# Attention ahead of a routed expert layer on one core: masks as TensorE products, plain row maxima moved within SBUF, no GpSimd work in the loop, K loaded once, heads normed in pairs

## The chip, the core and the metric

The kernel runs on one NeuronCore of a Trainium2 chip. TensorE multiplies matrices from SBUF into PSUM, VectorE (DVE) and ScalarE (ACT) do the elementwise work, GpSimd (POOL) is a fourth engine, SyncE (SP) issues transfers. Each engine executes its own instructions in the order in which the program was written; semaphores order them against each other. The metric is the time of one execution in microseconds on the device; the median of three runs is compared.

## What is computed

The first part is causal attention mixed with a recurrent memory, for 4 batches, 8 heads, 576 rows, head width 64:

```
scores = scale * np.matmul(q, k.transpose(0, 1, 3, 2))
scores = np.where(causal, -1000000000.0, scores)
scores = scores - scores.max(-1, keepdims=True)
a = np.exp(scores)
a /= a.sum(-1, keepdims=True) + 1e-09
local = np.matmul(a, v)
mem_ret = np.einsum('bhsd,bhde->bhse', q_p, M_prev)
mem_norm = np.einsum('bhsd,bhd->bhs', q_p, z_prev)[..., None] + 1e-06
return (g * mem_out + (1 - g) * local).astype(np.float32)
```

Here `q_p` is elu(q)+1, `mem_out` is `mem_ret / mem_norm` and `g` a sigmoid per head. Its 2304x512 result goes through a router that gives each of 8 experts 288 tokens (two 512x1024 layers each), and through a last layer with three 512x768 matrices, a maximum and a 768x512 matrix. All is float32; because the router's choices hang on small differences, products are split into a rounded part (fp32r) and a remainder.

## The kernel before

The 32 heads are worked off in 16 pairs. Of each pair the loop loads K and Q transposed (`Kr`, `Qr`, 64 rows, each written twice to fill 128 partitions), `QN` (Q again, for the memory), `MZ`, `V` and `VT`. ACT or DVE round Q and K to fp32r (`QX`, `KX`, `KB`), POOL computes the remainders (L436 into `KX`, L440 into `QL`).

Per head there are two passes over the scores. In the S pass (L480, and L482 for the last 64 rows of both heads together) TensorE computes score rows into one of three PSUM banks `s`, and DVE takes each row's maximum over score plus mask with one custom instruction (L499). The nine columns of maxima of a pair go out to DRAM, transposed element by element (L536, `nmd`), and come back as a row of `QL` (L543, L544), all on SP's queue. In the T pass (L598, L599) TensorE computes the transposed scores less the maxima into one of two banks `t`, ACT takes the exponential into `PT` (L609), POOL sets the upper triangle of the diagonal blocks to 0 (L627), and TensorE multiplies `PT` with `V` into one bank `av` per head (L642; a float32 product is two instructions). DVE divides by the row sums (L660 to L667) and adds to the batch's `x` (L671). The memory's products (L691) and the router's share of V (L383) have one bank, `mem`, in turn. After four pairs `x` is stored to DRAM (L801), from a tile whose rows of 64 elements lie 72 apart. Between these tasks 24 pieces of the last layer's float64 weights are loaded and turned to float32 (`m2raw`, L827 to L837).

The order on every engine comes from a planner (`Plan.run`): each task has engines it can run on with a cost, tasks it depends on, buffers from rings (`BUFS`), and a key (10 per pair, with offsets from `PRIO`). The planner takes the task that can start first, by key among equals, and writes the program in that order. The S pass has the offset -71 with six `KX`, so it runs about three pairs ahead of the T pass. Routing and the expert layer are planned apart, after it.

## Time and profile before

| | |
|---|---|
| Time, median of 3 runs (lowest, highest) | 1027.08 us (1024.65, 1042.5) |
| The profiled execution: its own time / its span | 1036.35 us / 1034.4 us |
| Busy: PE, PEld, DVE, ACT, POOL | 93%, 86%, 60%, 30%, 21% |
| Mean granted TensorE clock | 0.827 |
| DMA | 97.60 MB in 73339 packets, 46218 of them under 512 bytes |

The span is from the first to the last instruction. Busy shares are sums over stages: attention takes the time up to 425 us, the expert layer most of what follows. [...] A busy PE is one whose matmuls overlap in the record; how fast they follow one another is read from their starts.

### The profile page before, as it was taken

To read this page: it belongs to the slowest core of one execution; us is meant where nothing else is said; L and a number is where in the kernel's file an instruction comes from. 1 tells how busy PE (TensorE), PEld (TensorE's weight loads), DVE (VectorE), ACT (ScalarE), POOL (GpSimd) and SP (SyncE) were. 2 spreads that over 40 slices of the span, in tenths; PEclk is the share of its full clock that TensorE was granted. 3 is DMA by queue.
4 is the path that set the end of the run, shared out by engine and by line. 5 is a ranking of instruction groups with operands and counts; after the bars stand their busy time and mean duration, and the time that the engine had idled before them with its cause. 6 is when DMAs were issued, how large, how long until landed. Compare 5 with 4: busy or idle time off the path is not lost.

```text
span 1034.4 us, 17357 instructions
## 1 busy us (share of the span) xinstructions
PE 962.2 (93%) x6570; PEld 889.9 (86%) x6570; DVE 619.5 (60%) x1724; ACT 314.6 (30%) x678; POOL 216.9 (21%) x299
## 2 busy tenths in 40 slices
PE   7789998899989999668899999999989999999997
PEld 5679897789778878558899999999989999999996
DVE  8546656557774753588874775857727736253321
ACT  5223333224342322412223224223123133242311
...
GB/s 229 143 128 116 129 171 73 161 116 133 149 130 122 126 92 18 47 114 74 82 86 119 88 6 161 43 65 141 3 75 143 3 136 71 44 163 1 41 2 31
DMA packets 73339, 97.60 MB, mean 94 GB/s; under 512 B 46218, under 2 KB 48266, under 8 KB 73256
## 3 DMA queue, kind: packets, MB, share of 16 engines
...
## 4 chain that ended last, share of the span: by engine, by line
PE 60%; issue 14%; DMA 13%; DVE 9%; POOL 1%; SPq 1%; ACT 1%; POOLq 0%; DVEq 0%; ACTq 0%
PE av L642 9%; PE w L1270 8%; PE w L1272 8%; PE w L1271 8%; DMA m2raw<-in_m2w 4%; PE acc L1271 4%; PE acc L1270 4%; PE acc L1272 4%; DMA Qr<-in_qT 3%; PE t L598 3%; PE t L599 2%; PE s L480 2%; PE mem L691 2%; DMA Kr<-in_kT 2%; PE rps L1018 1%
## 5 line engine op out<-in xcount | busy, mean ns | idle before, releaser
L642 PEld LDWEIGHTS av<-V,PT 128*128 128x128 f32 (+2 forms) x960 | 167.1, 256 | 17.1 <-issue 5.6
L642 PE MATMUL av<-V,PT 128*128 128x73 f32 (+2 forms) x960 | 176.5, 347 | 0.0
L1270 PE MATMUL w<-yh,mh 128*128 128x288 f32 x576 | 174.4, 303 | 0.0
L1272 PE MATMUL w<-yh,ml 128*128 128x288 f32 x576 | 170.3, 296 | 0.0
L1271 PE MATMUL w<-yl,mh 128*128 128x288 f32 x576 | 170.0, 295 | 0.0
L1270 PEld LDWEIGHTS w<-yh,mh 128*128 128x128 f32 x576 | 109.3, 190 | 3.1
L1271 PEld LDWEIGHTS w<-yl,mh 128*128 128x128 f32 x576 | 109.0, 189 | 2.9
L1272 PEld LDWEIGHTS w<-yh,ml 128*128 128x128 f32 x576 | 108.9, 189 | 0.0
L1241 DVE TENSOR_TENSOR wlo<-wraw,whi 128x1024 fp32r<-128x1024 f32 x64 | 80.2, 1254 | 41.3 <-ACT whi L1237 41.2
L609 ACT ACTIVATE PT<-t 128x512 f32<-128x512 f32 x96 | 54.7, 595 | 157.2 <-PE av L642 95.1
L1204 POOL DMA_INDIRECT xg<-xd,tidx x24 | 23.8, 992 | 372.7 <-PE w L1272 181.9
L499 DVE CUSTOM_DVE_ANT_0 junk<-s,mask 128x256 bf16<-128x256 f32 (+4 forms) x145 | 73.4, 508 | 46.7 <-PE s L480 38.7
L1375 DVE TENSOR_TENSOR mt<-w,mt 128x288 f32<-128x288 f32 x96 | 43.8, 456 | 80.2 <-PE w L1272 76.1
L598 PE MATMUL t<-QX,KX 128*128 128x512 f32 (+4 forms) x160 | 75.1, 475 | 6.7 <-ACT PT L609 6.7
L1271 PE MATMUL acc<-hl,whi 128*128 128x288 f32 x256 | 77.6, 303 | 3.1 <-DVE hl L1178 2.7
L1270 PE MATMUL acc<-hh,whi 128*128 128x288 f32 x256 | 77.4, 302 | 2.8 <-ACT hh L1172 2.8
L1237 ACT CAST whi<-wraw 128x1024 fp32r<-128x1024 f32 x64 | 66.8, 1049 | 39.0 <-PE acc L1271 22.2
L1272 PE MATMUL w<-xhi,wlo 128*128 128x288 f32 x256 | 76.7, 300 | 1.1 <-DVE wlo L1241 1.1
L1270 PE MATMUL w<-xhi,whi 128*128 128x288 f32 x256 | 77.2, 301 | 0.0
L1271 PE MATMUL w<-xlo,whi 128*128 128x288 f32 x256 | 76.7, 299 | 0.0
L1272 PE MATMUL acc<-hh,wlo 128*128 128x288 f32 x256 | 76.3, 298 | 0.0
L627 POOL TENSOR_SCALAR_AFFINE_SELECT PT<-PT 128x256 f32<-128x256 f32 (+1 forms) x96 | 45.0, 476 | 148.5 <-ACT PT L609 137.6
...
## 6 DMA issues: line engine op xcount, KB each, us to landing
...
```

The lines of the kernel that those rows point to most:

```text
L499: V.tensor_tensor_reduce(out=junk[ps_, :z - a], in0=o.s[ps_, :z - a], in1=mask[ps_, k:k + z - a], scale=-0.125, scalar=init, op0=OP.add, o ...
L598: nc.tensor.matmul(o.t[:kr, c:c + z - a], r.KX[i][:, ks], r.QX[i][:, a:z], start=True, stop=False)
L609: A.activation(u.PT[:kr, at0:at0 + wd], o.t[:kr, :wd], AF.Exp, scale=0.125)
L627: G.affine_select(v, v, pattern=[[1, m]] if cnt == 1 else [[0, 2], [1, m]], compare_op=OP.is_ge, fill=0.0, base=0, channel_multiplier=-1)
L642: nc.tensor.matmul(av[:m, j], u.PT[:kr, o:o + m], r.V[:kr, kb, i], start=(kb == 0), stop=(kb == j))
L1204: g.gather = G.indirect_dma_start(out=x.xg[:96, c], out_offset=None, in_=xd, in_offset=bass.IndirectOffsetOnAxis(ap=r.tidx[:96, c:c + 1], ...
L1237: A.copy(x.W[fb][0], x.RAW[fb])
L1241: V.tensor_sub(x.W[fb][1], x.RAW[fb], x.W[fb][0].bitcast(F32))
L1270: nc.tensor.matmul(o, wh, rh, start=start, stop=False)
L1271: nc.tensor.matmul(o, wh, rl, start=False, stop=False)
L1272: nc.tensor.matmul(o, wl, rh, start=False, stop=stop)
L1375: V.tensor_max(q.mt, o.pt[:, :T], q.mt)
```

## The change

The attention part is written anew; routing and experts stay. Per pair and no longer per head:

- Masks: before each diagonal score product TensorE multiplies a bf16 identity with a bf16 mask into the same bank and the score product adds to it (L394, L403 in the S pass, L556 in the T pass). POOL's selection in `PT` is gone.
- Row maxima: DVE takes them with plain maximum reductions (L413), nine per pair, and one maximum joins the two parts of the last rows (L436). TensorE transposes the nine columns (L440), ACT copies them to SBUF and issues three transfers on its own queue that write them into the row of `QL` (L449, L450). The pass through DRAM is gone.
- `Kr` has 64 partitions and is loaded once; ACT rounds it (`KX`, `KB`) and Q, both heads in one instruction; DVE computes the remainders of both heads in one instruction each (L353, L358). POOL keeps one small copy per pair (`MZ`).
- Both heads have one buffer `av` of two banks; the division is done for both at once (L617 to L632). The memory's part of `x` is scaled by ACT, ten instructions per pair (L532). `x` is kept without the router's eight columns, which have a tile `g` of their own, so that the store's rows are 512 elements.
- The rings are shorter (`KX` 3, `QX` 3, `KB` 2 for pairs) and the S pass runs one pair ahead.

```diff
-PRIO = {'load': -12, 'phi': 2.0, 'min2': ['ACT'], 'prep': 7.5, 'cpe': ['ACT', 'DVE'], 'sube': ['POOL'], 'S': -71.0, 'J4': -2.0, 'R': -78.0, 'E': 29.0, 'N': -37.5, 'T': -3.0, 'A': 18.5, 'M': -60.0, 'rowe': ['ACT'], 'maske': ['POOL'], 'norm': 0.5, 'xadd': ['DVE'], 'mem': [0, 9], 'gate': 45.5, 'G': -13.0, 'gev': ['ACT'], 'm2': [15.0, 2, 25.0]}
+PRIO = {"load": -14, "prep": -12, "cb": 3, "S": -11, "N": -11, "nmte": "ACT", "G": -4, "phi": -6, "mem": (-2, -1), "memx": "ACT", "T": 0, "E": 0, "A": 4,
+        "norm": 4, "gate": -9, "m2": (4.0, 6.3, 6.0)}
...
-                for a in range(2):
-                    nc.sync.dma_start(t[64 * a:64 * a + 64], src[b, pp])
+            tK.append(load("Kr", [64, 2, S], kT[b, pp], k0 - 3 * (p == 0) + .01 * u, 1400 // len(parts), a, z, 1, u == 0))
...
-                copy(e, r.KX[i], r.Kr[:, i])
-                vg(e).tensor_sub(r.KX[i][64:], r.Kr[64:, i], r.KX[i][64:].bitcast(F32))
+                copy(e, r.KX[:64, s], r.Kr[:, s])
+                V.tensor_sub(r.KX[64:, s], r.Kr[:, s], r.KX[:64, s].bitcast(F32))
+                V.tensor_sub(r.QL[:64, s], r.Qr[:64, s], r.QX[:64, s].bitcast(F32))
...
-                V.tensor_tensor_reduce(out=junk[ps_, :z - a], in0=o.s[ps_, :z - a], in1=mask[ps_, k:k + z - a],
-                                       scale=-0.125, scalar=init, op0=OP.add, op1=OP.min, accum_out=acc)
+                        PE.matmul(o.s[:, c + z - a - 128:c + z - a], identb, ms[:, :128], start=True, stop=False,
+                                  skip_group_check=True)
+                        PE.matmul(d, r.QX[:, i, 128 * j:128 * j + 128], r.KX[:, i, a:z], start=False, stop=True,
+                                  skip_group_check=True)
+                    V.tensor_reduce(r.nm[:, col:col + k], o.s[:, c:c + k * w].rearrange("p (k w) -> p k w", k=k), axis=AX.X, op=OP.max)
...
-                nc.sync.dma_start(nmd[p].rearrange("c p -> p c"), u.nr.bitcast(F32))
-                    nc.sync.dma_start(q[:, :512], nmd[p:p + 1, 4 * i:4 * i + 4].rearrange("o c p -> o (c p)"))
-                    nc.sync.dma_start(q[:, 512:], nmd[p:p + 1, 8, 64 * i:64 * i + 64])
+            PE.matmul(r.pn[:9, :128], r.nm[:, :9], identr, start=True, stop=True)
+            copy(e, r.nmt, r.pn[:9, :128])
+            for i in range(2):
+                A.dma_start(q[:, i, :512], r.nmt[4 * i:4 * i + 4])
+            A.dma_start(q[:, :, 512:], r.nmt[8:9].rearrange("o (i q) -> o i q", i=2))
...
+                if diag:
+                    PE.matmul(o[:kr, c:c + kr], identb[:kr, :kr], mt[:kr, :kr], start=True, stop=False, skip_group_check=True)
...
-                    G.affine_select(v, v, pattern=[[1, m]] if cnt == 1 else [[0, 2], [1, m]], compare_op=OP.is_ge,
-                                    fill=0.0, base=0, channel_multiplier=-1)
...
+                for a in range(k):
+                    for i in range(2):
+                        A.mul(x[:, a, i], mv[:, a, i, :64], u.rm[:, a, i:i + 1])
...
-                    nc.sync.dma_start(xd[r].rearrange("p (h c) -> p h c", h=H), x[:rows(j), j, :, :64])
+                    nc.sync.dma_start(xd[r], x[:rows(j), j].rearrange("p h c -> p (h c)"))
```

How the order on TensorE changes, in the middle of the attention (`s`: S pass, `t`: T pass, `av`: PT times V, `mem`: memory and router products; sizes are partitions x columns). Before:

```order
L642 MATMUL av_108<-V,PT 128x73 x10
L691 MATMUL mem<-MZ,phi 128x146
L691 MATMUL mem<-MZ,phi 64x146
L642 MATMUL av_108<-V,PT 64x73 x5
L642 MATMUL av_109<-V,PT 128x73 x3
L480 MATMUL s<-KX,QX 128x128
L642 MATMUL av_109<-V,PT 128x73 x3
L480 MATMUL s<-KX,QX 128x256
L691 MATMUL mem<-MZ,phi 128x146 x3
L480 MATMUL s<-KX,QX 128x384
L598 MATMUL t<-QX,KX 128x320
L599 MATMUL t<-QL,KB_126 128x320
```

The products of the four kinds alternate. Now, from the end of one pair's `av` products to the first scores of the pairs behind it:

```order
L591 MATMUL av<-V,PT 128x73 x4
L591 MATMUL av<-V,PT 64x73 x5
L462 MATMUL mem<-wb,VT 128x16 x4
L462 MATMUL mem<-wb,VT 64x16
L591 MATMUL av<-V,PT 128x73 x10
L591 MATMUL av<-V,PT 64x73 x5
L509 MATMUL mem<-MZ,phi 128x146 x3
L394 LDWEIGHTS identb
L394 MATMUL s<-mask_s,identb 128x128
L396 MATMUL s<-KX,QX 128x512
L394 LDWEIGHTS identb
L394 MATMUL s<-mask_s,identb 128x128
```

Both heads' `av` products stand together, and the memory, S and T products, with the masks among them, stand together behind them. The T pass of the next pair follows a few rows on, also without `av` products between:

```order
L396 MATMUL s<-KX,QX 128x384
L556 LDWEIGHTS identb
L556 MATMUL t<-mask_t,identb 128x128
L557 MATMUL t<-QX,KX 128x512
L558 MATMUL t<-QL,KB_129 128x512
L557 MATMUL t<-QX,KX 128x64
L558 MATMUL t<-QL,KB_129 128x64
L556 LDWEIGHTS identb
L556 MATMUL t<-mask_t,identb 128x128
L557 MATMUL t<-QX,KX 128x448
L558 MATMUL t<-QL,KB_129 128x448
```

On SP's queue, before, at the end of a batch: the maxima's way through DRAM and the store of `x` stand among the loads, which wait behind them.

```order
L342 DMA QN<-in_qN 128x576
L536 DMA nmd<-nmr 128x9x1
L801 DMA xd<-x 1024x1x64 x4
L801 DMA xd<-x 512x1x64
L817 DMA m2raw<-in_m2w 128x1024
L543 DMA QL<-nmd 1x512
L544 DMA QL<-nmd 1x64
```

Now only loads and the store, in rows of 512 elements, are left on SP:

```order
L323 DMA Qr<-in_qT 64x1152 x2
L735 DMA m2raw<-in_m2w 128x1024
L717 DMA xd<-x 128x512 x4
L717 DMA xd<-x 64x512
L323 DMA MZ<-in_mz 128x146
L323 DMA V<-in_v 128x730
```

The maxima's transfers are now on ACT, behind the copy that they wait for, with the exponentials of the pair at work around them:

```order
L577 ACTIVATE PT<-t 128x512
L290 COPY nmt<-s 9x128
L532 ACTIVATE x<-mem,rm 128x64 x4
L449 DMA QL<-nmt 1x4x128 x2
L450 DMA QL<-nmt 1x2x64
L290 CAST qj_131<-Qr 128x2x64
L575 ACTIVATE PT<-t 64x2x64
```

Whatever stands behind these three on ACT, casts of the next pair and exponentials, is issued after them.

## Rows read from the trace of the kernel before

**Rows 1.** Busy time by stretch, attention: PEclk granted clock, DMA share, GB/s.
```profile
core 0: us, PE busy (x) PEld busy (x) DVE busy (x) ACT busy (x) POOL busy (x), PEclk, DMA share, GB/s
36.00:425.00 389.00, 361.29 (x1764) 320.69 (x1763) 226.38 (x646) 117.01 (x247) 131.31 (x186) 0.61 0.66 115
```
**Rows 2.** The same view, four shorter stretches of the attention.
```profile
120.50:164.80 44.30, 44.30 (x187) 39.59 (x186) 25.70 (x78) 13.18 (x30) 14.13 (x17) 0.50 0.64 136
250.20:267.20 17.00, 16.31 (x126) 14.53 (x124) 16.54 (x44) 8.61 (x18) 7.65 (x11) 1.00 1.08 160
265.00:270.00 5.00, 3.65 (x29) 3.05 (x28) 4.97 (x9) 2.17 (x5) 3.94 (x4) 1.00 0.98 206
396.00:416.00 20.00, 20.00 (x90) 17.79 (x91) 4.48 (x13) 4.10 (x9) 2.63 (x6) 0.50 0.00 0
```
**Rows 3.** The same view, the eight stretches at full clock: first, and their sum.
```profile
113.60:120.50 6.90, 6.43 (x52) 5.75 (x52) 6.52 (x16) 4.31 (x10) 4.46 (x6) 0.99 0.89 235
...
sum 85.50, PE 70.14 PEld 61.29 DVE 66.88 ACT 34.61 POOL 38.89; mean PE 8.77 PEld 7.66 DVE 8.36 ACT 4.33 POOL 4.86
```
**Rows 4.** Timeline of DVE: start us, us; division at a head's end (one per head).
```profile
63.63 0.52 DVE L667 TENSOR_TENSOR tmp<-av,r 128x360 f32<-128x360 f32 x1
...
119.32 0.53 DVE L667 TENSOR_TENSOR tmp<-av,r 128x360 f32<-128x360 f32 x1
...
144.74 0.53 DVE L667 TENSOR_TENSOR tmp<-av,r 128x360 f32<-128x360 f32 x1
...
254.80 0.53 DVE L667 TENSOR_TENSOR tmp<-av,r 128x360 f32<-128x360 f32 x1
...
263.87 0.52 DVE L667 TENSOR_TENSOR tmp<-av,r 128x360 f32<-128x360 f32 x1
...
424.93 0.53 DVE L667 TENSOR_TENSOR tmp<-av,r 128x360 f32<-128x360 f32 x1
```
**Rows 5.** Timeline of PE at either clock level.
```profile
102.51 1.82 PE L642 MATMUL av<-V,PT 128*128 128x73 f32 x8
104.07 0.45 PE L480 MATMUL s<-KX,QX 128*128 128x128 f32 x1
104.32 1.47 PE L691 MATMUL mem<-MZ,phi 128*128 128x146 f32 x4
...
114.88 1.01 PE L642 MATMUL av<-V,PT 128*128 128x73 f32 x8
115.70 0.30 PE L480 MATMUL s<-KX,QX 128*128 128x128 f32 x1
```
**Rows 6.** Busy time of L1217 (bf16 128x128 products, one after another) by stretch.
```profile
452.00:454.80 2.80, 2.80 (x29) 2.80 (x27) 0.50 1.09 41
455.20:458.00 2.80, 2.80 (x54) 2.80 (x52) 1.00 0.52 40
```
**Rows 7.** Groups by line and shape: count, busy us, mean ns; idle before, releasers.
```profile
L499 DVE CUSTOM_DVE_ANT_0 junk<-s,mask 128x512 bf16<-128x512 f32 x42 | 28.8, 685 | 15.5 <-PE s L480 9.3 <-PE s L482 6.0
L667 DVE TENSOR_TENSOR tmp<-av,r 128x360 f32<-128x360 f32 x32 | 16.9, 529 | 0.4
L609 ACT ACTIVATE PT<-t 128x512 f32<-128x512 f32 x90 | 51.2, 595 | 155.2 <-PE av L642 95.1 <-PE t L599 56.3 <-PE av L598 3.8
L406 DVE SCALAR_TENSOR_TENSOR phi<-QN,ph 128x576 f32<-128x576 f32 x2 | 1.5, 742 | 0.0
```
**Rows 8.** Timeline: a DVE and a POOL instruction that ran at one time.
```profile
264.83 1.41 POOL L440 TENSOR_TENSOR QL<-Qr,QX 64x576 fp32r<-64x576 f32 x1 [1.02 <-PE av L599]
264.88 1.98 DVE L406 SCALAR_TENSOR_TENSOR phi<-QN,ph 128x576 f32<-128x576 f32 x1
```
**Rows 9.** SP's queue: timeline, and waits of 36 to 425 us (total, times, longest).
```profile
256.55 10.62 SPq L801 DMA_DIRECT2D xd<-x  x5
...
SPq L543 <- DMA nmd<-nmr: 80.2, 13, 9.9
```
**Rows 10.** Timeline of PE just ahead of the clock's rise at 113.6 us.
```profile
109.93 1.76 PE L691 MATMUL mem<-MZ,phi 128*128 128x146 f32 x6
```

681 lines of the change are left out of this document (299 added, 382 removed).

## The prediction

> **What bounds the kernel now.** I read the busy times by stretch first, then the division at each head's end as a mark of pace, then TensorE's and DVE's timelines, then waits.
>
> Attention lasts to about 425 us; no line behind it changes, so its 609 us (1034.4 - 425) stay. From 36 to 425 us no engine is full except PE: 361 of 389 us busy at a granted clock of 0.61, DVE 226, ACT 117, POOL 131 [rows 1]. The mean hides two regimes [rows 2]. [...] The eight full-clock stretches sum to 85.5 us, 22% of the 389 [rows 3].
>
> The division at a head's end gives the pace [rows 4]: 25.4 us per pair at half clock (119.32 to 144.74), 9.07 us per head or 18.1 per pair at full (254.80 to 263.87), and 24.09 per pair over the fifteen pairs from 63.63 to 424.93. That is what has to shrink.
>
> **The change, part by part (per pair).**
>
> *TensorE.* Work goes up. Eight diagonal score blocks and one last pair block get a mask product in the S pass, ten blocks in the T pass: 19 products. The trace has no bf16 product among these. Nearest below are the bf16 128x128 products of the expert layer: 2.80 us / 29 = 0.097 us at half clock, 2.80 / 54 = 0.052 at full [rows 6]. Nearest above is the fp32r score product of 128 columns, which starts 0.25 us ahead of the next instruction at half clock [rows 5]. Each mask stands between products that load other weights, so I lean from the lower bound upward: 0.15 and, by the ratio below, 0.08. That is +2.9 us (1.8 to 4.8) at half clock and +1.5 at full; the transposition of the maxima adds 0.1. Eight `av` products take 104.07 - 102.51 = 1.56 us at half and 115.70 - 114.88 = 0.82 at full [rows 5], a ratio of 0.526. PE's work per pair is then 25.4 + 3.0 = 28.4 us at half clock (27.3 to 30.3) and 25.4 x 0.526 + 1.6 = 15.0 at full.
>
> *DVE.* Nine reductions of 3136 columns in all replace the custom maxima; POOL's two remainders come to DVE; the casts of K and Q leave it. From 360 elements in 529 ns, 512 in 685 (from PSUM) and 576 in 742 [rows 7] an instruction costs about 160 ns + 1.02 ns per element. Reductions: 9 x 0.16 + 3.2 = 4.6, and 0.2 for the maximum that joins two. Remainders: two of 1152, 2.7. Division and additions for both heads: 1460 elements in five instructions, 2.3. `phi` 0.75; the memory's divisors, six small ones, 1.1; 1.5 weight pieces of three instructions of 512, 3.1. Sum 14.8 us. Before it was 226.38 / 16 = 14.1, part of it stretched by POOL: 1.98 us for the `phi` instruction that ran beside L440 [rows 8], against 742 ns alone [rows 7]. That stretch goes.
>
> [...]
>
> *ACT.* 117.01 / 16 = 7.3 now [rows 1]. It takes all of the K and Q casts: 3456 columns at 595 ns per 512 [rows 7] are 4.0 at most, and about half of them were its own before, so +2. Ten scalings of 64 columns lie between 595 x 64 / 512 = 0.07 and 0.595 us each, 0.7 to 6.0; such a narrow one is mostly fixed cost, like DVE's 0.16, so I take 0.21 each, 2.1. The copy of the maxima 0.25. What three issues of transfers hold ACT no row shows; from nothing to 0.5 each, I take 0.25, 0.75. Sum 12.4, at the upper bounds 17: then ACT would be the bound at full clock, near the 17.5 below.
>
> *SP and DMA.* The store of `x` held SP's queue 10.6 us per batch, and the waits for the maxima's way out summed to 80.2 us in 13 [rows 9]; loads stood behind both. Both leave. K's second copy goes (64 x 1152 floats, 0.29 MB per pair). Where PE is the bound this is worth nothing now; it feeds the full-clock stretches, where the DMA share was 1.08 [rows 2].
>
> *The maxima's hop.* The three transfers are on ACT behind the copy; casts and exponentials are queued behind them, and the first remainder product of the T pass waits for them. The S pass is one pair ahead, and the 40 `av` instructions of the pair between give a cover of 40 x 0.195 = 7.8 us at half clock, 4.1 at full [rows 5], and the memory and score products on top. A hop of 2 to 3 us (an estimate from 6.2 us per wait for the hop through DRAM, which has two legs [rows 9]) is hidden. Were it not, 3 us x 15 pairs = 45 us come back.
>
> **The sum.** If the clock stayed as it is at half, the change loses 28.4 - 25.4 = 3 us per pair. At full clock the largest of PE 15.0, DVE 14.8, ACT 12.4 bounds a pair; with the waits that three nearly equal engines cause on each other I take 17.5 (18.1 was the best before). So the result hangs on f, the share of attention's time at full clock: a pair lasts P = 1 / (f / 17.5 + (1 - f) / 28.4). Attention changes by 15 x (P - 24.09); before, f was 0.22.
>
> | f | P | change | time |
> |---|---|---|---|
> | 0 | 28.4 | +65 | 1092 |
> | 0.22 | 25.0 | +13 | 1040 |
> | 0.50 | 21.7 | -36 | 991 |
> | 0.75 | 19.4 | -70 | 957 |
> | 1 | 17.5 | -99 | 928 |
>
> The profiled run took 1036.35 us (1034.4 span and 2 around it), 0.9% above the median 1027.08; I work the change out in its trace and take it from the median.
>
> Why f should rise: the order now puts memory, score, mask and T products of a pair in one stretch, and the `av` products, whose inputs lie ready, in another. Before, the clock rose at 113.6 us, 2 us behind a run of memory products [rows 10], while in 396 to 416 us, mostly `av` and T in turn, with PE busy 20.00 of 20.00 and no DMA at all, it stayed at 0.50 [rows 2]: a busy PE alone did not bring the rise there, and what stood ahead of one was such a run. It fell where PE waited for DVE, POOL or loads [rows 2]; these waits shrink, since POOL's share, SP's waits and DRAM leave the chain. Against: DVE and ACT have more work each, three engines are near equal at full clock, and PE will still wait. I take f = 0.5.
>
> **Rivals.**
>
> 1. *The clock rises half of the time* (f from 0.40 to 0.75): 957 to 1007 us. For it: the above. Chance 0.40; point 990.
>
> 2. *Full clock nearly throughout* (f over 0.75): 928 to 957. For it: no more SP or POOL waits. Against: DVE at 14.8 us of 17.5 leaves little slack, and each wait of PE was followed by a fall. Chance 0.20. [...]
>
> 3. *The clock stays as it is* (f from 0.19 to 0.40): masks and clock about cancel, 1007 to 1045. For it: PE was full before without the clock rising. Chance 0.18.
>
> 4. *The hop of the maxima is late*: the gain of f = 0.5 is eaten by 45 us, about 1035. For it: ACT issues it between exponentials, in its order. It decides from 2.4 us per pair on. Chance 0.07.
>
> 5. *Slower* (f under 0.19): TensorE has 3 us more per pair and its work is what bounds at half clock; if the waits at pair ends keep it there, 1047 to 1092. The point from which this decides is f = 0.19, close to the 0.22 of before. Chance 0.15.
>
> About 2% (20.5 us) is what a measurement of this kernel can tell from no change. Faster by more (f over 0.40 without a late hop): 0.60. Within: 0.25. Slower: 0.15. The range reaches from f = 0.93 (935) to f = 0.18 (1048), which leaves about 0.09 below and 0.11 above.
>
> **What would show it.** The granted clock of the attention (0.61 before): 0.75 at f = 0.5. The pace of the division: 21 to 22 us per pair; 28 in stretches at 0.50, 17 to 18 at 1.00. A reduction of 512 columns near 0.69 us; if it takes twice that, DVE is the bound at 19 us. A mask product 0.10 to 0.25 us ahead of its score product at half clock. No store over 5 us and no wait on `nmd` on SP. T's products with `QL` waiting on transfers would show rival 4, ACT at 15 us per pair a wrong price of its issues or scalings. I am wrong in kind if the clock share is about as before and the time still falls by 30 us, or if it rises and the time does not fall.

## The result: 930 us, under the range

The changed kernel takes 930.34 us (median of 4 runs, 928.14 to 935.49). The runs of before that stood beside them have a median of 1034.79 us; the ratio is 0.9076, with a 95% interval of 0.901 to 0.9142. The prediction said 990, with a range of 935 to 1048. The time is 60 us under the point and 5 us under the range. A single execution of these kernels can take a few per cent longer at a lower granted clock (before, on the chip of e14: 1066 to 1073 us at 0.79 to 0.81, beside 1046 to 1051 us at 0.82 to 0.83); the differences below are taken between executions without this. It lies where rival 2 was put ("full clock nearly throughout", 928 to 957, chance 0.20).

The profiled execution took 935.49 us with a span of 933.8, against 1034.4: 100.6 us less. The table shows where they went; the marks are the first instruction of the program, the division that ends pair 0, the division that ends pair 15, and the end.

| stretch | before, us | after, us | difference |
|---|---|---|---|
| start to the end of pair 0 | 63.6 | 55.2 | -8.4 |
| fifteen pairs | 361.3 (24.09 each) | 272.5 (18.17 each) | -88.8 |
| behind attention | 609.5 | 606.0 | -3.4 |

The sums are from [rows 4] and from these rows, the division on DVE now (start us, us, instruction; one per pair, and one per head for the last pair):

```profile
55.24 0.91 DVE L624 TENSOR_TENSOR tmp<-av,r 128x720 f32<-128x720 f32 x1
...
94.29 0.91 DVE L624 TENSOR_TENSOR tmp<-av,r 128x720 f32<-128x720 f32 x1
111.47 0.91 DVE L624 TENSOR_TENSOR tmp<-av,r 128x720 f32<-128x720 f32 x1
128.77 0.91 DVE L624 TENSOR_TENSOR tmp<-av,r 128x720 f32<-128x720 f32 x1
...
327.76 0.53 DVE L624 TENSOR_TENSOR tmp<-av,r 128x360 f32<-128x360 f32 x1
```

At full clock a pair lasts 17.2 us (94.29 to 111.47, and again to 128.77). Busy time by stretch of the changed kernel answers [rows 1] and [rows 2]: the whole attention, 20 us at full clock, and one of the falls.

```profile
core 0: us, PE busy (x) PEld busy (x) DVE busy (x) ACT busy (x) POOL busy (x), PEclk, DMA share, GB/s
36.00:331.00 295.00, 289.97 (x2099) 244.02 (x2099) 196.59 (x474) 175.84 (x409) 8.46 (x46) 0.90 0.49 143
...
100.00:120.00 20.00, 20.00 (x156) 16.13 (x155) 15.78 (x40) 13.71 (x32) 0.20 (x1) 1.00 0.66 194
160.00:166.60 6.60, 6.60 (x33) 6.08 (x32) 2.66 (x5) 2.70 (x4) 0.00 (x0) 0.50 0.39 113
```

The granted clock of the attention, as a share of full speed, is 0.90 where it was 0.61. The records of before and after have two levels of it, 0.50 (44.30 us at a stretch in [rows 2]) and 1.00 (the 20.00 us above), so the share of time at full clock is f = 2 x clock - 1: 0.80 now, 0.22 before. PE is busy 289.97 of 295 us, and 20.00 of 20.00 at full clock, where before it waited (3.65 of 5 in [rows 2]). The DMA share fell from 0.66 to 0.49 while the rate rose from 115 to 143 GB/s. That last pair of numbers turned out to be the clue.

### The profile page after: what moved, and what is told of

The parts are those of the page before. It is cut to its first block, busy times and chain, and to the rows that moved or that the text cites. A ratio compares the mean times of both kernels' runs of the same rounds, so it can differ in the third digit from the quotient of the medians.

```text
span 933.8 us, 17447 instructions
## 1 busy us (share of the span) xinstructions
PE 889.8 (95%) x6880; PEld 811.5 (87%) x6880; DVE 572.9 (61%) x1481; ACT 365.2 (39%) x826; POOL 80.0 (9%) x145
## 4 chain that ended last, share of the span: by engine, by line
PE 76%; issue 14%; DVE 4%; POOL 1%; DMA 1%; ACT 1%; ACTq 1%; SPq 1%; POOLq 0%; DVEq 0%
PE av L591 12%; PE w L1187 9%; PE w L1189 9%; PE w L1188 9%; PE acc L1188 4%; PE acc L1187 4%; PE acc L1189 4%; PE t L557 4%; PE mem L509 3%; PE t L558 3%; PE s L396 3%; PE rps L935 2%; PE mem L462 1%; PE t L556 1%; PE s L400 1%
## 5 line engine op out<-in xcount | busy, mean ns | idle before, releaser
L591 PE MATMUL av<-V,PT 128*128 128x73 f32 (+2 forms) x960 | 128.4, 286 | 1.6 <-ACT PT L575 0.7
L591 PEld LDWEIGHTS av<-V,PT 128*128 128x128 f32 (+2 forms) x960 | 116.1, 194 | 9.0 <-ACT PT L575 1.5
L1292 DVE TENSOR_TENSOR mt<-w,mt 128x288 f32<-128x288 f32 x96 | 43.6, 454 | 80.2 <-PE w L1189 78.0
L577 ACT ACTIVATE PT<-t 128x512 f32<-128x512 f32 x96 | 56.6, 609 | 87.0 <-PE t L558 85.8
L1154 ACT CAST whi<-wraw 128x1024 fp32r<-128x1024 f32 x64 | 66.8, 1049 | 40.3 <-PE acc L1188 22.2
L413 DVE TENSOR_REDUCE nm<-s 128x1 fp32r<-128x512 f32 (+4 forms) x160 | 69.1, 471 | 13.9 <-PE s L396 11.7
L1054 ACT CAST gc<-mt 128x32 fp32r<-128x32 f32 (+2 forms) x72 | 17.5, 243 | 143.4 <-DVE mt L1292 143.4
L557 PE MATMUL t<-QX,KX 128*128 128x512 f32 (+2 forms) x192 | 70.0, 366 | 0.0
L1095 DVE SCALAR_TENSOR_TENSOR hl<-w,hh 128x288 fp32r<-128x288 f32 x64 | 29.0, 455 | 63.3 <-ACT hh L1089 61.3
```

The source lines that it names most:

```text
L413: V.tensor_reduce(r.nm[:, col:col + k], o.s[:, c:c + k * w].rearrange("p (k w) -> p k w", k=k), axis=AX.X, op=OP.max)
L557: PE.matmul(d, r.KX[:, i, ks_], r.QX[:, i, a:z], start=not diag, stop=False, skip_group_check=True)
L577: A.activation(r.PT[:, items[0][0], out:out + 512], o.t, AF.Exp, scale=0.125)
L591: PE.matmul(av[:m, i, j], r.PT[:kr, i, o:o + m], V4()[:kr, kb, i], start=kb == 0, stop=kb == j)
L1095: V.scalar_tensor_tensor(lo(), src(), 0.0, hi().bitcast(F32), op0=OP.max, op1=OP.subtract)
L1154: A.copy(x.W[fb][0], x.RAW[fb])
```

## Where the loss of before sat, read again

Busy time of before by short stretches, about one of the stores of the maxima (issued by SP at 207.6 us), and a stretch without one:

```profile
204.00:208.00 4.00, 4.00 (x19) 3.91 (x18) 4.00 (x9) 0.81 (x2) 3.37 (x6) 0.50 0.53 114
208.00:212.00 4.00, 4.00 (x22) 3.64 (x21) 0.96 (x4) 0.00 (x0) 0.38 (x1) 0.50 1.10 9
212.00:216.00 4.00, 4.00 (x20) 3.75 (x19) 2.16 (x8) 1.66 (x3) 0.41 (x1) 0.50 0.56 34
248.00:252.00 4.00, 4.00 (x28) 3.76 (x27) 2.69 (x9) 0.69 (x1) 1.84 (x2) 0.73 0.98 287
```

From 208 to 212 us the DMA engines' mean busy share is 1.10 and they move 9 GB/s; from 248 to 252 nearly the same share (0.98) moves 287. The store transposes 9 x 128 values element by element, so it is 1152 writes of 4 bytes. The packets recorded from 208 to 210, from 210 to 219 and from 219 to 222 us:

```profile
DMA packets 1178, 0.03 MB, mean 13 GB/s; under 512 B 1168, under 2 KB 1168, under 8 KB 1178
DMA packets 120, 0.23 MB, mean 25 GB/s; under 512 B 10, under 2 KB 10, under 8 KB 120
DMA packets 421, 0.84 MB, mean 282 GB/s; under 512 B 53, under 2 KB 181, under 8 KB 420
```

The single elements are recorded within two us; for the nine us behind them the larger packets of the transfers issued next move at 25 GB/s, and then at 282. How the store holds up what comes behind it, the record does not show. The chain of waits of before, from 205 to 225 us (start us, us, what), shows what that costs TensorE:

```profile
208.72 12.84 DMA m2raw<-in_m2w
...
221.66 0.09 ACT m2a L827
...
222.24 0.59 ACT PT L609
222.83 0.04 issue
222.87 0.42 PE t L598
```

and the row of PE's timeline that it leads to, with the like rows at two other falls:

```profile
35.47 2.21 PE L383 MATMUL mem<-wb,VT 128*128 128x16 f32 x10 [1.10 <-DVE x L710]
177.37 0.85 PE L691 MATMUL mem<-MZ,phi 128*128 128x146 f32 x2 [3.33 <-ACT V L292]
222.87 0.42 PE L598 MATMUL t<-QX,KX 128*128 128x64 f32 x1 [2.09 <-ACT PT L609]
```

A weight piece issued at 208.7 us lands after 12.84 us. ACT is idle for 7.30 us ahead of L827, which reads it; the exponential L609, next in ACT's order, starts 0.58 us behind L827's start, and the T product that needs its bank starts behind that. PE was idle for 2.09 us there, and at 223 us the clock, which had been at full for 3.5 us, fell to 0.50. So a late load of the last layer's weights, which attention does not need at all, stopped attention, and the clock then stayed at half for 27 us (to 250) although PE was busy again, 27.20 of 27.20 us from 222.90 to 250.10. Of the eight falls after 36 us in the attention of before, five stand where ACT waited for a load: 3.3 to 7.6 us for a weight piece (192, 223, 318 and 370 us), 4.2 us for `V` (175, where PE was idle for 3.33 us). Two stand behind 1.36 us of PE's waiting for DVE's L710 (271 and 305), and one behind 0.47 us (120). A ninth, at 35 us, stands behind 1.10 us of waiting for L710.

By the full-clock stretches that [rows 3] adds up, the clock was at half for 303.5 of the 389 us: 151 us behind the five falls at a late load, 78 behind the fall at 35 us, 48 behind the one at 120, and 27 behind the other two. So half of the half-clock time begins at a late load. Why the clock then stays at half for tens of us under a busy PE, no run here shows.

The group of L827 and its counterpart, over the attention (count, busy us, mean ns, idle before it us and what ended it), before and after:

```profile
L827 ACT ACTIVATE m2a<-m2raw 128x512 f32<-128x512 f32 x24 | 16.2, 676 | 34.9 <-DMA m2raw<-in_m2w 30.2 <-DMA m2raw<-in_m2wo 4.5
```

```profile
L745 ACT ACTIVATE m2a<-m2raw 128x512 f32<-128x512 f32 x24 | 16.5, 687 | 0.6 <-DMA m2raw<-in_m2w 0.6
```

34.9 us of idle ACT became 0.6.

## The experiments

Four theories stood at first: A, the order on TensorE brings the clock (the prediction's); B, TensorE no longer waits for others; C, the mask products themselves lift the clock; and, after the first results, D, the way of the maxima. Each experiment was run beside the kernel before on the same chip; before took 1042 to 1073 us on these chips, more than the 1025 to 1047 of the runs above, so times are compared within a chip. The changed kernel itself stood beside them on one chip only (e14, 0.9016 of before, where the result has 0.9076). The clock is that of the attention, from 36 us to its end, and the pace is the mean of the fifteen pairs behind pair 0.

### The order (theory A)

**The products spread among each other (e1).** Only keys of the planner change; T, score and `av` products alternate.

```diff
-PRIO = {"load": -14, "prep": -12, "cb": 3, "S": -11, "N": -11, "nmte": "ACT", "G": -4, "phi": -6, "mem": (-2, -1), "memx": "ACT", "T": 0, "E": 0, "A": 4,
+PRIO = {"load": -20, "prep": -19, "cb": 3, "S": -18, "N": -8, "nmte": "ACT", "G": -4, "phi": -6, "mem": (-2, -1), "memx": "ACT", "T": 0, "E": 0, "A": 4,
...
-            piece(ks + .1 * i, [(3, i, 0, 512, 0, True)], [(0, 512, 1, 4 * i + 3, 0)])
+            piece(ks + 1.2 * i, [(3, i, 0, 512, 0, True)], [(0, 512, 1, 4 * i + 3, 0)])
...
-                ex[i, gi] = score(n + 3 * i + .1 * gi, [(i, gr)], 512 * gi)
+                ex[i, gi] = score(n + 5 * i + 1.3 * gi, [(i, gr)], 512 * gi)
...
-                outs.append(add(n + 3 * i + W["A"] + .1 * j, {"PE": (168, 382, 596, 810, 628)[j]}, fAV(i, j),
+                outs.append(add(n + 5 * i + W["A"] + 1.0 * j, {"PE": (168, 382, 596, 810, 628)[j]}, fAV(i, j),
...
-        kq = n + 3 + W["norm"]
+        kq = n + 5 + 4 + W["norm"]
```

> The changed kernel, with nothing changed but the planner's keys: score, T, memory and av products of a pair are spread among each other (runs of at most ten av instructions between T and score products) instead of standing in two blocks. Same instructions, same buffers, same transfers. Theory A (the order brings the clock): the granted clock of the attention falls from about 0.87 to 0.55 to 0.70, the pace goes from 17.2 to 22 to 26 us per pair, the time to 990 to 1050. Theory B (the clock is up because TensorE no longer waits for POOL, SP and DRAM): the clock stays at 0.85 or more and the time within 920 to 945.

Measured: 904.26 and 929.56 us, and the clock did the opposite of what theory A asks. Busy time by stretch of this kernel:

```profile
36.00:299.00 263.00, 261.84 (x2090) 223.25 (x2089) 196.71 (x453) 170.90 (x406) 7.67 (x46) 1.00 0.57 158
60.00:80.00 20.00, 20.00 (x159) 17.18 (x159) 14.93 (x36) 12.83 (x30) 1.07 (x1) 1.00 0.59 166
```

It rose at 33 us and did not fall once before 299. The pace is 16.40 us per pair. Theory A falls: the two blocks are not what brings the clock; they cost some of it.

**The kernel before, with its products grouped (e3).** The planner's keys of before are set so that T products of both heads stand together and `av` products behind them.

```diff
-PRIO = {'load': -12, 'phi': 2.0, 'min2': ['ACT'], 'prep': 7.5, 'cpe': ['ACT', 'DVE'], 'sube': ['POOL'], 'S': -71.0, 'J4': -2.0, 'R': -78.0, 'E': 29.0, 'N': -37.5, 'T': -3.0, 'A': 18.5, 'M': -60.0, 'rowe': ['ACT'], 'maske': ['POOL'], 'norm': 0.5, 'xadd': ['DVE'], 'mem': [0, 9], 'gate': 45.5, 'G': -13.0, 'gev': ['ACT'], 'm2': [15.0, 2, 25.0]}
+PRIO = {'load': -12, 'phi': 2.0, 'min2': ['ACT'], 'prep': 7.5, 'cpe': ['ACT', 'DVE'], 'sube': ['POOL'], 'S': -11, 'J4': -2.0, 'R': -78.0, 'E': 29.0, 'N': -37.5, 'T': -3.0, 'A': 3, 'M': -60.0, 'rowe': ['ACT'], 'maske': ['POOL'], 'norm': 0.5, 'xadd': ['DVE'], 'mem': [0, 9], 'gate': 45.5, 'G': -13.0, 'gev': ['ACT'], 'm2': [15.0, 2, 25.0]}
...
-                piece(n + j, (i,), j, 0, 128 * j + 128, True, True, ttr[-1:])
+                piece(n + .1 * j, (i,), j, 0, 128 * j + 128, True, True, ttr[-1:])
...
-        n = r.n + 5 * i
+        n = r.n + .5 * i
```

> The kernel before, with only its planner's keys changed: T products of both heads at one key, av products right behind (offset 3 for 18.5), score products one pair ahead, so that av products stand in runs of 12 to 24 and score, T and memory products in runs between. POOL's masks and remainders, the maxima's way through DRAM and K's second copy stay. Theory A: the granted clock of the attention rises from 0.61 to 0.75 or more and the time falls to 960 to 1000. Theory B: the waits stay, so the clock stays near 0.6, and the time is 1020 to 1060.

Measured: 1073.6 and 1066.86 us (before beside it 1050.63), clock 0.61 as before. Grouping alone brings nothing; this kernel is slower than before by 2% (0.5 to 3.5).

**Two score products between the heads' `av` products (e4).**

```diff
-PRIO = {"load": -14, "prep": -12, "cb": 3, "S": -11, "N": -11, "nmte": "ACT", "G": -4, "phi": -6, "mem": (-2, -1), "memx": "ACT", "T": 0, "E": 0, "A": 4,
+PRIO = {"load": -14, "prep": -16, "cb": 3, "S": -11, "N": -11, "nmte": "ACT", "G": -4, "phi": -6, "mem": (-2, -1), "memx": "ACT", "T": 0, "E": 0, "A": 4,
...
-            piece(ks + .1 * i, [(3, i, 0, 512, 0, True)], [(0, 512, 1, 4 * i + 3, 0)])
+            piece(ks - 3.2 + .1 * i, [(3, i, 0, 512, 0, True)], [(0, 512, 1, 4 * i + 3, 0)])
```

> The changed kernel, with two 512-column score products of the pair ahead (and the router's five small ones) moved between the av products of the first and the second head, by the planner's keys alone. All six falls of the clock in the changed kernel lie in runs of av products (at 71, 160, 197, 235, 272 us and at the end). Theory A: such a run is now broken, falls become fewer than four, and the time is 915 to 926. Theory B: falls have nothing to do with the place of the score products: 926 to 936.

Measured: 914.93 and 955.57 us. In the profiled execution (the former) the clock was 0.96 and fell three times before the end. Two runs 40 us apart decide nothing beside 930; the profile only agrees with shorter `av` runs losing the clock less often.

### The mask products (theory C)

**Without them, in the order of the change (e2).** The products L394, L403 and L556 are taken out, and with them the causal mask.

```diff
-                        PE.matmul(o.s[:, c + z - a - 128:c + z - a], identb, ms[:, :128], start=True, stop=False,
...
-                        PE.matmul(d, r.QX[:, i, 128 * j:128 * j + 128], r.KX[:, i, a:z], start=False, stop=True,
+                        PE.matmul(d, r.QX[:, i, 128 * j:128 * j + 128], r.KX[:, i, a:z], start=True, stop=True,
...
-                                      stop=h == 1 and not diag)
-                        if diag:
-                            PE.matmul(d, identb, ms[:, 128:], start=False, stop=True)
...
-                if diag:
-                    PE.matmul(o[:kr, c:c + kr], identb[:kr, :kr], mt[:kr, :kr], start=True, stop=False, skip_group_check=True)
-                PE.matmul(d, r.KX[:, i, ks_], r.QX[:, i, a:z], start=not diag, stop=False, skip_group_check=True)
+                PE.matmul(d, r.KX[:, i, ks_], r.QX[:, i, a:z], start=True, stop=False, skip_group_check=True)
```

> The changed kernel without its 19 mask products per pair, so the causal mask is left out of the computation. Theory A: the clock stays (0.87 of attention at full), and what goes is the products' own 19 x 0.039 us = 0.7 us per pair: about 918 us. Theory C (the dense bf16 mask products are what lifts the clock): the granted clock falls towards the 0.61 of before, and the time rises to 960 or more in spite of less work. By the price of the prediction (0.08 each at full) the gain would be 1.6 us per pair, 905 us.

Measured: 937.83 and 945.83 us; clock 0.81, f = 0.62. Less work, and no gain: beside the changed kernel (clock 0.88 to 0.90) more time went by at half clock.

**Without them, in the spread order (e6).** Both edits, that of e1 and that of e2, together.

> The spread order of the first experiment without the 19 mask products per pair (the causal mask is left out). Theory C: without them the clock no longer holds: share at full clock under 0.7 and time 930 to 1000. Theory B, or a clock that simply stays up once it has risen in this order: share 0.95 or more, and about 0.7 us per pair less than the spread order, 890 to 905 us.

Measured: 891.38 and 910.21 us; clock 0.95, pace 15.66 us against 16.40 with masks. This kernel spent 24 us at half clock, from 171 to 195 us, so the two paces are not at one clock. Seven pairs ran at full clock in both; e1 first, then this one:

```profile
53.15:172.69 119.54, 119.54 (x956) 102.06 (x954) 93.35 (x212) 79.48 (x188) 2.44 (x6) 1.00 0.65 180
51.44:159.82 108.38, 106.46 (x822) 94.76 (x821) 91.99 (x213) 78.56 (x187) 2.98 (x6) 1.00 0.72 198
```

That is 17.08 us per pair with masks and 15.48 without: 1.60 less, 0.084 per product. The masks cost time here; but the clock fell once without them, where it did not fall with them.

**Added to the kernel before (e5).**

```diff
-                        nc.tensor.matmul(o.s[:, :z - a], r.QX[i][:, 128 * j:128 * j + 128], r.KX[i][:, a:z], start=True, stop=True)
+                        nc.tensor.matmul(o.s[:, z - a - 128:z - a], identb, warm[:, :128], start=True, stop=False, skip_group_check=True)
+                        nc.tensor.matmul(o.s[:, :z - a], r.QX[i][:, 128 * j:128 * j + 128], r.KX[i][:, a:z], start=False, stop=True,
...
-                    nc.tensor.matmul(o.t[:kr, c:c + z - a], r.KX[i][:, ks], r.QX[i][:, a:z], start=True, stop=False)
-                    nc.tensor.matmul(o.t[:kr, c:c + z - a], r.KB[i][:65, ks], r.QL[i][:65, a:z], start=False, stop=True)
+                    dg = a == 128 * kb
+                    if dg:
+                        nc.tensor.matmul(o.t[:kr, c:c + kr], identb[:kr, :kr], warm[:kr, :kr], start=True, stop=False, skip_group_check=True)
+                    nc.tensor.matmul(o.t[:kr, c:c + z - a], r.KX[i][:, ks], r.QX[i][:, a:z], start=not dg, stop=False, skip_group_check=True)
+                    nc.tensor.matmul(o.t[:kr, c:c + z - a], r.KB[i][:65, ks], r.QL[i][:65, a:z], start=False, stop=True, skip_group_check=True)
```

> The kernel before, with 18 bf16 128-column products per pair added (an identity times a tile of zeros, into the same banks, at the places where the changed kernel has its masks); POOL's and DVE's masks stay, so it computes the same. Order and all else as before. Theory C (the mask products lift the clock): the granted clock of the attention rises from 0.61 to 0.70 or more, and the time falls by 15 us or more although TensorE has more work. Theory B (the clock is up because TensorE no longer waits): the clock stays near 0.61, and 18 x 16 products of 0.074 us at half and 0.039 us at full clock add about 18 us.

Measured: 1063.55 and 1092.5 us against 1043.6. The former is 20 us over before, so work alone was added; the profile, of the latter, has a clock of 0.59. Theory C is no cause of the gain. In both orders of the changed kernel the clock was lower without masks (0.81 for 0.88 to 0.90 in e2, 0.95 for 1.00 in e6); two runs of each don't settle whether the masks hold some of it.

### The way of the maxima (theory D)

**Through DRAM again, in the changed kernel (e7).**

```diff
-            PE.matmul(r.pn[:9, :128], r.nm[:, :9], identr, start=True, stop=True)
...
-            copy(e, r.nmt, r.pn[:9, :128])
+            nc.sync.dma_start(nmd[p].rearrange("c p -> p c"), r.nm[:, :9].bitcast(F32))
...
-                A.dma_start(q[:, i, :512], r.nmt[4 * i:4 * i + 4])
-            A.dma_start(q[:, :, 512:], r.nmt[8:9].rearrange("o (i q) -> o i q", i=2))
+                nc.sync.dma_start(q[:, i, :512], nmd[p:p + 1, 4 * i:4 * i + 4].rearrange("o c p -> o (c p)"))
+                nc.sync.dma_start(q[:, i, 512:], nmd[p:p + 1, 8, 64 * i:64 * i + 64])
```

> The changed kernel with the maxima's way as before: stored to DRAM transposed and loaded back, all on SP's queue. Theory B (waits of SP and the hop held the clock down): TensorE waits again at pair ends, the share at full clock falls under 0.6, and the time rises to 970 or more. If the hop is hidden behind the pair in between, the time stays within 925 to 945.

Measured: 1066.35 and 1059.3 us, 1.0175 of before (1.0072 to 1.0277); clock 0.68, attention to 456 us. With this one part undone, the whole gain is gone.

**Within SBUF, in the kernel before (e9).** The reverse: of the whole change only this.

```diff
-                nc.sync.dma_start(nmd[p].rearrange("c p -> p c"), u.nr.bitcast(F32))
...
+                nc.tensor.matmul(u.pn[:9, :128], u.nr[:, :9], identr, start=True, stop=True)
...
+                copy(e, u.nmt, u.pn[:9, :128])
...
-                    nc.sync.dma_start(q[:, :512], nmd[p:p + 1, 4 * i:4 * i + 4].rearrange("o c p -> o (c p)"))
-                    nc.sync.dma_start(q[:, 512:], nmd[p:p + 1, 8, 64 * i:64 * i + 64])
...
+                    A.dma_start(q[:, :512], u.nmt[4 * i:4 * i + 4])
+                    A.dma_start(q[:, 512:], u.nmt[8:9, 64 * i:64 * i + 64])
```

> The kernel before with one part of the change alone: the nine columns of maxima are transposed by TensorE, copied by ACT and written into the row of QL by transfers on ACT's queue, instead of through DRAM on SP's queue. Theory D (the way through DRAM and the queue of loads that waits behind it are what held the kernel before): the 80 us of SP's waits go, the share at full clock in the attention rises from 0.22 to 0.4 or more and the time falls by 30 us or more. Theory E (with the score pass three pairs ahead the way through DRAM was covered, and it only hurts in the new structure, one pair ahead): within 15 us of before.

Measured: 973.66 and 947.72 us. The latter stands against a median of 1049.62 for before on the same chip: 102 us less, about what the whole change brings (104 us in the result). The profile is that of the execution of 973.66 us, attention and the group of the weight pieces:

```profile
36.00:365.00 329.00, 312.58 (x1802) 277.04 (x1800) 230.96 (x659) 121.31 (x265) 128.75 (x185) 0.73 0.50 135
L835 ACT ACTIVATE m2a<-m2raw 128x512 f32<-128x512 f32 x24 | 16.1, 670 | 7.5 <-DMA m2raw<-in_m2w 5.9 <-DVE m2b L839 0.8 <-DMA m2raw<-in_m2wo 0.6
```

f is 0.46 where it was 0.22, and ACT's idle time ahead of the weight pieces 7.5 us where it was 34.9. POOL's work, K's second copy, the old order and the store of `x` in rows of 256 bytes are all still there.

**Through DRAM, on ACT's queue (e10).** The edit is shown against e7.

```diff
-            nc.sync.dma_start(nmd[p].rearrange("c p -> p c"), r.nm[:, :9].bitcast(F32))
+            A.dma_start(nmd[p].rearrange("c p -> p c"), r.nm[:, :9].bitcast(F32))
...
-                nc.sync.dma_start(q[:, i, :512], nmd[p:p + 1, 4 * i:4 * i + 4].rearrange("o c p -> o (c p)"))
-                nc.sync.dma_start(q[:, i, 512:], nmd[p:p + 1, 8, 64 * i:64 * i + 64])
+                A.dma_start(q[:, i, :512], nmd[p:p + 1, 4 * i:4 * i + 4].rearrange("o c p -> o (c p)"))
+                A.dma_start(q[:, i, 512:], nmd[p:p + 1, 8, 64 * i:64 * i + 64])
```

> As the run with the maxima through DRAM in the changed kernel (1063 us), but with its five transfers on ACT's queue, so that no load waits behind them. Theory D1 (the loads behind the waits on SP's queue are the harm): the time comes back to 930 to 950. Theory D2 (the two legs and the 1152 single-element writes of each pair are late themselves): TensorE waits for QL, and the time stays over 1000; ACT's exponentials, queued behind, would be late too.

Measured: 1077.62 and 1080.31 us. Loads no longer stand behind the waits on SP's queue, and it is no better. ACT, though, stands behind the store itself now (53.0 us of waiting at `QX` alone), so this run alone does not settle D1; e11 bears on it.

**Within SBUF, on SP's queue (e11).**

```diff
-                A.dma_start(q[:, i, :512], r.nmt[4 * i:4 * i + 4])
-            A.dma_start(q[:, :, 512:], r.nmt[8:9].rearrange("o (i q) -> o i q", i=2))
+                nc.sync.dma_start(q[:, i, :512], r.nmt[4 * i:4 * i + 4])
+            nc.sync.dma_start(q[:, :, 512:], r.nmt[8:9].rearrange("o (i q) -> o i q", i=2))
```

> The changed kernel with its three transfers of the maxima within SBUF issued on SP's queue instead of ACT's. Theory D1 (loads wait on SP behind the maxima): SP waits for the copy of the maxima once per pair, the loads behind are late by as much, and the time rises to 960 or more. Theory D2: the transfer is short on any queue, 925 to 945.

Measured: 910.49 and 949.85 us, one below and one above the 928 to 935 of the result. SP waits 21.4 us for the copy of the maxima here, with the loads behind it, and these runs show no loss by it.

**The single-element writes alone (e12).** The changed kernel with the old store added; nobody reads `nmd`.

```diff
+        def fd(e):
+            nc.sync.dma_start(nmd[p].rearrange("c p -> p c"), r.nm[:, :9].bitcast(F32))
...
+        add(kn, {"SP": 300}, fd, [t], use=[bf["nm"]])
```

> The changed kernel, which keeps its way of the maxima within SBUF, with the old transposing store to DRAM added on SP's queue (9 x 128 single elements per pair). Nothing reads what it writes. Theory D3 (the 1152 writes of 4 bytes occupy the DMA engines, so that the loads come late): most of the loss comes back, the time is 1000 or more. Theory D4 (the latency of the two legs is the harm): nobody waits for it, so 925 to 950.

Measured: 1050.92 and 1067.24 us. The former is 108 us over the 942.46 of the changed kernel on the same chip, for 16 stores whose result nobody reads. This is the experiment that decides: nothing but the store was added. Two things come with it on SP's queue, 30.5 us of waits ahead of the stores, and loads that by the profile wait for the store to land, 46.5 us in all, most of them at L323:

```profile
SPq L323 <- DMA nmd<-nm: 36.9, 7, 7.8
```

How much of the 108 us is theirs was not separated; e11 with 21.4 us of such waits shows no loss, and e13 below, where SP waits 48.1 us, loses some 32. What the store does without that queue is seen on ACT's. Busy time by stretch of this kernel, behind a store issued at 151.4 us and behind one issued at 179.8:

```profile
154.00:158.00 4.00, 4.00 (x36) 3.79 (x35) 0.77 (x1) 2.33 (x3) 0.00 (x0) 1.00 0.64 28
158.00:162.00 4.00, 3.15 (x24) 2.25 (x23) 0.96 (x3) 0.00 (x0) 0.00 (x0) 1.00 0.78 27
162.00:166.00 4.00, 0.00 (x0) 0.00 (x0) 0.11 (x1) 0.11 (x1) 0.00 (x0) 0.66 0.54 160
...
186.00:190.00 4.00, 4.00 (x20) 3.92 (x20) 1.35 (x1) 1.48 (x4) 0.00 (x0) 0.50 0.97 29
```

the packets recorded from 152 to 154 and from 154 to 163 us:

```profile
DMA packets 1177, 0.01 MB, mean 7 GB/s; under 512 B 1175, under 2 KB 1175, under 8 KB 1177
DMA packets 54, 0.22 MB, mean 25 GB/s; under 512 B 0, under 2 KB 0, under 8 KB 54
```

and its chain of waits from 150 to 170 us:

```profile
152.93 13.73 DMA QL<-nmt
166.67 0.04 issue
166.71 0.79 PE t L562
```

and PE's timeline at that place:

```profile
160.68 0.47 PE L561 MATMUL t<-QX,KX 128*128 128x512 f32 x1
166.71 0.79 PE L562 MATMUL t<-QL,KB 65*128 65x512 f32 x1 [5.56 <-DMA QL<-nmt]
```

For nine us behind the single elements the engines move 25 GB/s. The transfers of the maxima within SBUF, on another queue, come 13.73 us after their issue. PE is idle for 5.56 us, to 166.7, and the clock falls from 1.00 to 0.50 in that gap; it comes back only at 197. From 186 to 190 PE is busy 4.00 of 4.00 at half clock: that is what a "wholly busy" PE at 0.50 looks like behind a late transfer.

**Through DRAM in whole rows (e13).** The maxima are transposed by TensorE first, and stored as nine rows of 512 bytes.

```diff
-                A.dma_start(q[:, i, :512], r.nmt[4 * i:4 * i + 4])
-            A.dma_start(q[:, :, 512:], r.nmt[8:9].rearrange("o (i q) -> o i q", i=2))
+                nc.sync.dma_start(q[:, i, :512], nmd[p:p + 1, 4 * i:4 * i + 4].rearrange("o c p -> o (c p)"))
+                nc.sync.dma_start(q[:, i, 512:], nmd[p:p + 1, 8, 64 * i:64 * i + 64])
...
+            nc.sync.dma_start(nmd[p], r.nmt)
```

> The changed kernel with the maxima still transposed by TensorE and copied by ACT, but then stored to DRAM in nine whole rows of 512 bytes and loaded back, all on SP's queue. Theory D3 (only the single-element writes do harm): 925 to 950 like the changed kernel. If the latency of the two legs and the waits on SP's queue do harm too: 970 or more.

Measured: 981.32 and 968.32 us; clock 0.79. With the single elements gone, most of the loss is gone; some 32 us stay against the 943.29 (median) of the kernel with K loaded twice, below, on the same chip. SP waits, in this kernel, for the copy of the maxima (total us, times, longest):

```profile
SPq L453 <- ACT nmt L290: 48.1, 13, 17.9
```

Whether these waits or the second leg make the 32 us was not tried.

So theory B holds in the form of D: the waits that went are those for loads and transfers behind these stores (PE is busy 289.97 of 295 us in the changed kernel). B does not tell why the clock can also fall without such a wait.

### Other parts of the change

**The remainders on POOL (e8).**

```diff
-                V.tensor_sub(r.KX[64:, s], r.Kr[:, s], r.KX[:64, s].bitcast(F32))
+                vg(e).tensor_sub(r.KX[64:, s], r.Kr[:, s], r.KX[:64, s].bitcast(F32))
...
-                V.tensor_sub(r.QL[:64, s], r.Qr[:64, s], r.QX[:64, s].bitcast(F32))
+                vg(e).tensor_sub(r.QL[:64, s], r.Qr[:64, s], r.QX[:64, s].bitcast(F32))
...
+            tsk.append(add(k + .02, {"POOL": 3180} if p else {"DVE": dve(w)}, sk, [tck[u]], use=U_("Kr", "KX")))
...
+            tsq.append(add(k + W["cb"] + .01, {"POOL": 3180} if p else {"DVE": dve(w)}, sq, [tcq[u]], use=U_("Qr", "QX") + ([] if not u else U_("QL")), **N_("QL")))
```

> The changed kernel with the remainders of K and Q back on POOL (both heads in one instruction, from the second pair on). By the prediction DVE has 2.7 us per pair less of its own and POOL's instructions, of about 3.2 us each, stretch DVE's that run beside them. Theory B (POOL's part in the chain held the clock down): the share at full clock falls and the time rises by 20 us or more. Otherwise within 10 us of the changed kernel's 930.

Measured: 942.21 and 946.2 us, clock 0.90 as in the changed kernel. POOL is busy 82 us in the attention and DVE 24 less; neither is the bound.

**K loaded twice (e17).**

```diff
-            tK.append(load("Kr", [64, 2, S], kT[b, pp], k0 - 3 * (p == 0) + .01 * u, 1400 // len(parts), a, z, 1, u == 0))
+            tK.append(load("Kr", [128, 2, S], kT[b, pp], k0 - 3 * (p == 0) + .01 * u, 2200 // len(parts), a, z, 2, u == 0))
...
-                copy(e, r.KX[:64, s], r.Kr[:, s])
+                copy(e, r.KX[:64, s], r.Kr[:64, s])
...
-                V.tensor_sub(r.KX[64:, s], r.Kr[:, s], r.KX[:64, s].bitcast(F32))
+                V.tensor_sub(r.KX[64:, s], r.Kr[:64, s], r.KX[:64, s].bitcast(F32))
...
-                copy(e, r.KB[:64, s], r.Kr[:, s])
+                copy(e, r.KB[:64, s], r.Kr[:64, s])
```

> The changed kernel with K loaded twice again (0.29 MB more per pair, as rows of 4608 bytes). By the prediction worth nothing: 925 to 950. If every load on the DMA engines counted as the single-element writes did: 960 or more.

Measured: 946.32 and 940.26 us; clock 0.90, DMA share 0.58 for 0.49. 4.7 MB more in whole rows cost nothing that can be seen (0.8985 of before); 74 kB in single elements cost 108 us.

### A version that beats both

On one chip, with three rounds: the changed kernel (e14), the spread order (e15), and the spread order (e16) with more filling products at the start, shown against e15:

```diff
-FILL = 48
+FILL = 80
```

> The changed kernel itself once more, beside the two following on one chip: 925 to 940, share at full clock in the attention 0.75 to 0.95.

> The spread order of the first experiment, timed. If the clock stays up in this order once it has risen (1.0 in the profile of e1), the median is 900 to 915, 15 us or more under the changed kernel beside it. If that was one lucky execution (the other gave 929.6), the two are alike.

> The spread order with 80 instead of 48 of the filling products at the start, which the planner puts into TensorE's idle time from 14 to 25 us, where the clock fell in all profiles so far. If the clock then stays at full from 6 us on: 8 to 12 us less than e15, about 895. If the filling products are in the way of pair 0: as e15 or some us more.

| kernel | median us (lowest, highest) | ratio to before, interval | attention's clock |
|---|---|---|---|
| changed kernel | 942.46 (941.79, 952.71) | 0.9016 (0.8915, 0.9116) | 0.88 |
| spread order | 908.26 (906.02, 909.59) | 0.8652 (0.8614, 0.8691) | 1.00 |
| spread, more filling | 909.75 (906.67, 910.97) | 0.8671 (0.8621, 0.8720) | 1.00 |

The spread order is 34 us under the changed kernel: its clock rises at 33 us and holds, and a pair takes 16.4 us for 18.9. The filling products move the first fall of the clock from 16 to 21 us and gain nothing: the rise came at 32 us in place of 33.

```profile
36.00:299.70 263.70, 262.34 (x2095) 223.76 (x2093) 197.42 (x454) 171.35 (x406) 7.44 (x46) 1.00 0.56 158
```

## Why the prediction was wrong, step by step

**SP and DMA: the step that failed.** "Where PE is the bound this is worth nothing now" was said of the removed waits, stores and copies together. For K's second copy it held (e17). For the way of the maxima it missed by 102 us (e9), and 108 in the other direction (e12). The prediction looked at the 80.2 us of SP's waits [rows 9] as a matter of SP's queue, and asked who stands behind it there; e11 shows no loss by the queue, and e13 leaves 32 us to it at most. What matters most is what the store does to the transfers behind it. Short stretches show it, by the rate beside the share. The 46218 packets under 512 bytes in the table of before are no proof by themselves: many are the 256-byte rows of `x`, and e9 still has 17189 small ones from 36 to 320 us (25068 before) without that loss. The prediction wrote of "the full-clock stretches, where the DMA share was 1.08 [rows 2]" (at 160 GB/s) and did not ask how many GB/s such a share moved elsewhere: 9 GB/s at 1.10 from 208 to 212 us. The trace had the size too: behind a store of 4.5 kB the rate was 25 GB/s for nine us, and the waits for such a store reached 9.9 us [rows 9].

**What bounds the kernel: right in the rows, wrong in what they mean.** PE was busy 44.30 of 44.30 us at 0.50 [rows 2], and the prediction took its work for "what bounds at half clock". It was, for those 44 us. But the clock had gone to half earlier, in five of the eight falls at a gap behind a late load; from then on a busy PE at half clock looks like a kernel that has no other trouble. The chain, of which each link has its row above for the fall at 223 us, is: single-element store, late weight piece, ACT in order, late exponential, idle PE, clock down, PE busy at half speed. That the store set off each of the other falls at a late load is argued from this one and from e9 and e12, not shown fall by fall.

**Why f should rise: one reason wrong, one right and priced too low.** The order was made responsible first. In the spread order f was 1.00, with the grouped order on the kernel before 0.22. The run of memory products ahead of the rise at 113.6 us [rows 10] was an accompaniment. The second reason, that PE's waits for loads shrink with SP's waits and DRAM, is what came true, and it got f = 0.5. "Each wait of PE was followed by a fall" was read too far: at 294.83 us of before PE had waited 1.15 us, and the clock stayed at full to 304.8. That "a busy PE alone did not bring the rise there" holds for 396 to 416 us of before (20.00 of 20.00 us at 0.50, [rows 2]) as for 186 to 190 us of e12 (4.00 of 4.00 us at 0.50). But with the waits gone and the work spread the clock was at full from 33 to 300 us (e15, PE busy 262.34 of 263.70 us from 36 us on). Rival 2 was the right case and got 0.20.

**The sum over f: right.** With f over the fifteen pairs as measured (36.3 of 272.5 us at half, f = 0.867) the formula gives 1 / (0.867 / 17.5 + 0.133 / 28.4) = 18.4 us per pair; 18.17 were measured. So -85 of the -88.8 us follow from the formula, and the mis-sized term is f: 0.50 taken, 0.87 measured. At full clock 17.5 was taken and 17.2 measured.

**The start was not priced.** 8.4 us of the gain lie ahead of the end of pair 0. The prediction took the fifteen pairs for the whole. With the right f alone the forecast would have been 1027 - 85 = 942 us, within the range; these 8.4 and the 3.4 us behind attention take it to 930.

**TensorE's work: right in the masks, and two errors that cancelled.** The masks were taken at 0.15 and 0.08 us. The matmuls' timeline at half and at full clock (start us, us):

```profile
30.55 0.33 PE L394 MATMUL s<-mask_s,identb 128*128 128x128 bf16 x1
30.64 0.67 PE L396 MATMUL s<-KX,QX 128*128 128x384 f32 x1
...
94.33 0.22 PE L394 MATMUL s<-mask_s,identb 128*128 128x128 bf16 x1
94.36 0.47 PE L396 MATMUL s<-KX,QX 128*128 128x512 f32 x1
94.68 0.23 PE L394 MATMUL s<-mask_s,identb 128*128 128x128 bf16 x1
```

From start to start they take 0.09 and 0.04 us, less than the lower bound at full (0.052, [rows 6]). But that is not their whole price: with them a pair at full clock takes 1.60 us more (e1 against e6), 0.084 each, as was forecast. PE's whole work at full clock was forecast as 15.0 us per pair, with 2.5 us of waits on top. It is 17.2, and PE is busy 20.00 of 20.00 there: the waits did not occur, the work was 2.2 us more, and that 17.5 came out is luck. Why the sum, scaled from a half-clock stretch of one pair, fell short was not tried. At full clock TensorE, not three engines in a draw, is the bound.

**DVE and ACT: near.** Groups of the changed kernel over the attention:

```profile
L413 DVE TENSOR_REDUCE nm<-s 128x1 fp32r<-128x512 f32 x43 | 28.8, 670 | 2.1 <-PE s L396 1.8 <-PE s L400 0.3
...
L532 ACT ACTIVATE x<-mem,rm 128x64 f32<-128x64 f32 x155 | 34.9, 319 | 0.9 <-DVE g L522 0.7 <-PE s L403 0.2
```

A reduction of 512 columns takes 670 ns (0.69 forecast), as long as the custom instruction's 685 [rows 7]. There are ten per pair, not nine (160 in 16 pairs): nine columns of maxima, one of them joined from two. DVE is busy 196.59 / 16 = 12.3 us per pair, 14.8 forecast. ACT's scalings cost 319 ns each (0.21 taken) and each issue of a transfer about 0.6 (0.25 taken); with 175.84 / 16 = 11.0 us busy and 1.8 us of issues ACT is at 12.8, 12.4 forecast.

**The hop: right.** In the changed kernel's attention TensorE waited for `QL` once, 0.6 us (a weight load of L558); rival 4 did not occur. The cover is longer than counted, 60 `av` instructions per pair and not 40 (960 in 16 pairs). The hop is short, though, only while no single-element store stands ahead of it (13.73 us in e12).

**Rivals 3 and 5** asked for a clock as before. They did not occur, but e12 shows how near they lay: with the old store added, the changed kernel takes 1051 us, and before takes 1049 on that chip.
